# A fused attention and gated-convolution kernel: its tables split into pieces, scores of batch 0 on half the rows per head, weight loads placed between the staged loads, loads of later batches spaced

## The chip, the cores and the metric

The kernel runs on one core of a Trainium2 chip. The metric is the device time of one execution in microseconds (us). Three executions of the kernel before are known: 435.98, 435.8 and 434.76 us, median 435.8.

A core has five engines that run their own instruction queues in order and wait for each other by semaphores: TensorE (PE, matmuls), VectorE (DVE), ScalarE (ACT), GpSimd (POOL) and SyncE (SP, which here only issues transfers). Transfers are issued by SP or POOL and carried out by 16 DMA engines.

## What is computed

Attention with one added to the softmax's denominator, then a gated long convolution by Fourier transform, cut to its core:

```python
# q, k, v: (8, 12, 448, 64) float32; w_proj (768, 2304), filter_fft (448, 768), w_out (768, 768)
scores = q @ k.T / sqrt(64)
m = max(scores);  e = exp(scores - m)
attn = e / (sum(e) + exp(-m) + 1e-9)
x = (attn @ v) as (8, 448, 768)
x1, x2, x3 = split(x @ w_proj, 3)
conv = irfft(rfft(x2, axis=1) * rfft(filter_fft, axis=0))
out = (x1 * conv * x3) @ w_out          # (8, 448, 768) float32
```

## The kernel before

**Units.** The twelve heads of a batch are taken in six pairs; pairs are numbered through the batches (`i` or `g`, 0 to 47). A pair's attention (`attention(i)`) has four `scores` steps on PE into PSUM: one matmul of 448 columns for the 64 keys left over of both heads (`t` = 0), and for `t` = 1 to 3 two matmuls, one per head, each with 128 keys and all 128 rows of the two heads' features. So that a head doesn't see the other's features, POOL first spreads q into a tile `qz` that is zero in the other head's 64 rows (`spread`, two copies; three such tiles in turn, so `qz` of pair i waits for the scores of pair i-3). ACT takes the exponentials (`exps`), PE multiplies with v (`attn_out`, two halves), DVE divides (`norm`) into `xb`, and `xb` is transposed into `xT`: by PE and a DVE copy for all of batch 0 and the last pair of a batch, by a transposing DMA from SP for the others (`x_dma`).

**The dense part** (`dense(b)`) needs `xT` of all six pairs. DVE folds it (`first`, `second`: a copy of two columns, sums and differences) into `xf`; PE projects (`proj2`, eight chunks P of six matmuls with the weight part 1), turns the result into a spectrum (`spectrum`), DVE multiplies by the filter's spectrum `hrs`, PE transforms back (`inverse`); PE makes the gates x1 and x3 straight from `xT` (`gate`, weight parts 0 and 2); DVE multiplies, PE projects with `wout_bf`, ACT copies out, SP stores.

**Loads.** Batches 0 and 1 are staged (`staged(b)`): SP loads a pair's k, q and v as float32 into one of three slots of `nat`, and `rests`, the left-over keys and values, once a batch. Casts to bfloat16 follow (k and q on DVE, but q of pairs 1 to 5 on POOL; v on POOL), then PE transposes k and q (`turn`), and two copies bring them to `kT` and `qT`. Batch 1 loads q in rows of 1 KB (four sequence rows at once), and ACT puts the columns in order while it copies. Batches 2 to 7 (`loaded(b)`) are cast in the transfer by 13 DMAs from POOL, and transposed by DMAs from SP (`q_turn`, four, and `k_turn`, six a batch). They need room in `nat`, which the transposes of the batch before give.

**Weights and tables.** `wproj_bf` comes in three parts, `filt` and `wout_bf` in one each, from POOL, each at a time after a cast of some v. The Fourier tables (`tables`, `more_tables`) are written at the start outside the planner, almost all on DVE: phases, a sine on ACT, `half`, `jm`, `ft`, `bt`, and on PE and ACT the mirrored `fr`.

**What sets the order.** All work is handed to a planner (`Plan`) as tasks with an engine, a cost, a due time (`want`), what they need and make, and buffers they take and give; `after` is an earliest time. It plays the tasks through by its own costs and writes down each engine's order; on the chip nothing of the times is left, only the order and the waits. `tau(i)` is the due time of pair i, `PERIOD` 46 for a batch.

Of the kernel before, what the change touches and what calls it, by code (L numbers as in the profile page):

```python
# [11 lines left out]
AF = mybir.ActivationFunctionType  # L12
# [8 lines left out]
SP = 112  # L21
# [20 lines left out]
class Plan:  # L42
# [17 lines left out]
    def run(self):  # L60
# [14 lines left out]
        rings = {"SP": 0.0, "POOL": 0.0}  # L75
# [22 lines left out]
        while any(queue.values()):  # L98
            moved = False
            for e in queue:  # L100
# [17 lines left out]
                if dma:  # L118
                    other = rings["SP" if e == "POOL" else "POOL"]
                    begin = max(rings[e], end)  # L120
                    rings[e] = begin + dma * (1.6 if other > begin else 1.0)
                    end = rings[e] + 1.8
# [23 lines left out]
def kernel(  # L146
# [14 lines left out]
    NSTAGED = 2  # L161

# [47 lines left out]

    def stage(g, at, n):
        o = (g % 3) * SLOT + at
        return nf[:, o : o + n]
# [10 lines left out]
    ATT0, SLOT0, PERIOD = 7.5, 3.5, 46.0  # L224
    BASE = ATT0 + 6 * SLOT0

    def tau(i, frac=0.0):

        i += frac
        return ATT0 + SLOT0 * i if i < NHP else BASE + (i - NHP) * PERIOD / NHP  # L230

# [11 lines left out]
    def staged(b):  # L243


        for hp in range(NHP):
            g = b * NHP + hp
            want = tau(g) - (8.0 if b == 0 else 12.0)
            natural = b == 0
            for n, (name, x) in enumerate((("k", k), ("q", q), ("v", v))):  # L250
                src = stage(g, (0, 768, 384)[n], (384, 512, 384)[n])

                def load(name=name, x=x, src=src, hp=hp):
                    if name == "q" and natural:
# [5 lines left out]
                    elif name == "q":  # L260
                        nc.sync.dma_start(
                            src[0:SP].rearrange("p (u c) -> p u c", u=2),
                            x[b, 2 * hp : 2 * hp + 2].rearrange("u (p j) d -> p u (j d)", j=NST),
                        )
# [5 lines left out]
                add("SP", 1.0 if name == "q" and natural else 0.45, want + 0.1 * n, load, need=[("c" + name, g - 3)] if g >= 3 else (),  # L270
                    make=[("s" + name, g)],
                    dma=1.6 if name == "q" and natural else 0.8)
                if hp == 0 and name != "q":
                    add("SP", 0.45, want + 0.1 * n + 0.15,
                        lambda n=n, x=x: nc.sync.dma_start(rests[:, n // 2], shared(x, b)),
                        need=[("cr" + name, b - 1)] if b else (), make=[("r" + name, b)], dma=0.75)

                def cast(name=name, src=src, hp=hp, g=g):
                    if name == "k":
                        T[g]["kn"] = t = ld.tile([128, 3, 128], BF16, name="k0")  # L280
                        nc.vector.tensor_copy(
# [3 lines left out]
                    elif name == "q":  # L285
                        T[g]["qn"] = t = ld.tile([SP, NST, 2, DH], BF16, name="q0")
                        (nc.gpsimd if natural and hp else nc.vector).tensor_copy(
# [11 lines left out]
                if name == "v":  # L299
                    add("POOL", 0.75, tau(g) + 1.0, cast, need=[("sv", g)], make=[("cv", g), ("v", g)])  # L300
                else:
                    on_pool = name == "q" and natural and hp > 0
                    add("POOL" if on_pool else "DVE", 0.8 if on_pool else 0.45, tau(g) - (2.0 if b == 0 else 5.0), cast, need=[("s" + name, g)], make=[("c" + name, g)],
                        after=tau(g) - (4.0 if b == 0 else 7.0) if g >= 3 else 0.0,
                        take=[(name + "0", g)])
            if hp == 0:
                for u in range(2):
                    c = slice(64 * u, 64 * u + 64)
                    add("DVE", 0.25, want + 6.0, lambda c=c: nc.vector.tensor_copy(ks[c, :, c], rests[c, 0]),
                        need=[("rk", b), "zero ks"] + ([("T", NHP * b - 1)] if b else []), make=[("crk", b)])  # L310
                    add("POOL", 0.5, tau(g) + 1.0,
# [20 lines left out]
            def q_back(g=g, hp=hp):  # L332
                tb = T[g]["ps"].bitcast(BF16)
                if natural:
# [711 lines left out]
```

## Time and profile before

| | us |
|---|---|
| three executions | 434.76 to 435.98, median 435.8 |
| the profiled execution | 433.81 |
| its span, first to last instruction | 432.0 |
| PE busy | 394.7 (91%) |
| DVE, ACT busy | 274.7 (64%), 275.3 (64%) |
| POOL busy | 164.5 (38%) |

Times below are from the profiled execution, counted from the span's start. A line of the timeline gives start, duration, engine, line of the source, operation, the tiles it writes and reads, and in brackets the engine's idle time before it with what ended it. In lines of groups stand the count, the total, the mean in ns, and the idle time before. PE's clock is given as a share of full speed.

### The profile page before, as it was taken

The numbers are of one execution on the slowest core, as the hardware profiler recorded it, in microseconds if no ns is written. First come the engines' busy times: TensorE is split into PE (matmuls) and PEld (weight loads), VectorE is DVE, ScalarE is ACT, GpSimd is POOL, SyncE is SP. The second block draws the span as 40 slices with busy tenths as digits, with TensorE's granted clock in tenths as the row PEclk, the third lists the DMA queues.
The fourth block names the chain that finished last, engine by engine and source line by source line (L and its number), as shares of the span: only waits on it lengthen the run. The fifth ranks groups of instructions, "written<-read, shape, count | busy, mean of one in ns | idle before, by whom it ended". The sixth has DMA issues, their size and how long they took to land.

```text
span 432.0 us, 9027 instructions
## 1 busy us (share of the span) xinstructions
PE 394.7 (91%) x3401; PEld 262.3 (61%) x3401; DVE 274.7 (64%) x782; ACT 275.3 (64%) x460; POOL 164.5 (38%) x257
## 2 busy tenths in 40 slices
PE   1795689979898899999999999999999999999995
PEld 1463457646574566766676667666766667666562
DVE  7585546784564845787567844884689457764660
ACT  3584548747666566776767776777687666753433
POOL 7872340955657431681456234814131121000000
PEclk9998879989999899999999999999999999999999
DMA  8999971999999969992999299917970220102004
GB/s 204 215 230 231 249 139 31 107 142 159 189 143 143 102 135 149 134 122 46 203 130 114 42 177 179 139 18 145 137 79 14 86 86 14 26 14 109 3 0 146
DMA packets 178011, 51.09 MB, mean 118 GB/s; under 512 B 163373, under 2 KB 174384, under 8 KB 177968
## 3 DMA queue, kind: packets, MB, share of 16 engines
q0 software_dynamic: 101680, 17.80, 61.3%
q1 hardware_dynamic: 76288, 32.72, 39.3%
q8 instruction: 26, 0.43, 0.4%
q14 instruction: 17, 0.14, 0.1%
HBM read 43.86 MB, written 11.01 MB: 127 GB/s over the span
## 4 chain that ended last, share of the span: by engine, by line
PE 80%; DMA 8%; DVE 6%; issue 2%; ACT 2%; POOL 1%; SPq 0%; DVEq 0%; POOLq 0%; ACTq 0%
PE pps L809 22%; PE pps L736 14%; PE ops L904 12%; PE sc L583 11%; PE op L616 7%; DMA xT<-xb 5%; PE cps L843 4%; DMA nat<-in_v_dram 3%; PE op L611 2%; PE xsp L763 2%; PE sc L585 2%; ACT e L591 1%; DVE t L777 1%; PE tps L324 1%; PE xps L665 1%
## 5 line engine op out<-in xcount | busy, mean ns | idle before, releaser
L591 ACT ACTIVATE e<-sc 128x896 bf16<-128x896 f32 x144 | 129.9, 919 | 42.5 <-PE sc L583 41.6
L809 PE MATMUL pps<-xT,wproj_bf 128*128 128x448 bf16 x576 | 122.5, 353 | 1.8 <-DMA xT<-xb 1.0
L572 POOL COPY qz<-qT 64x448 bf16<-64x448 bf16 x96 | 60.9, 634 | 113.9 <-PE sc L583 82.5
L583 PE MATMUL sc<-qz,kT 128*128 128x448 bf16 x288 | 80.2, 367 | 8.7 <-POOL qz L572 8.6
L809 PEld LDWEIGHTS <-wproj_bf 128*128 128x128 bf16 x576 | 55.7, 98 | 49.8 <-issue 3.1
L736 PE MATMUL pps<-wproj_bf,xf 128*113 128x384 bf16 x384 | 72.2, 331 | 0.6 <-ACT xs L771 0.4
L616 PE MATMUL op<-vn,e 128*128 128x65 bf16 x1152 | 59.2, 195 | 0.9 <-ACT e L591 0.6
L736 PEld LDWEIGHTS <-xf 128*113 128x113 bf16 x384 | 50.7, 134 | 15.4 <-issue 1.4
L616 PEld LDWEIGHTS <-e 128*128 128x128 bf16 x1152 | 51.8, 99 | 7.8 <-ACT e L591 1.4
L904 PE MATMUL ops<-wout_bf,yT 128*128 128x384 bf16 x288 | 51.4, 326 | 0.0
L629 DVE TENSOR_SCALAR rec<-op 128x4 f32<-128x4 f32 x96 | 15.2, 158 | 56.8 <-PE op L616 56.5
L821 ACT CAST x<-pps 128x448 bf16<-128x448 f32 x48 | 25.7, 535 | 38.8 <-PE pps L809 35.7
L611 PE MATMUL op<-vr,er 128*128 128x130 bf16 x192 | 42.5, 221 | 3.7 <-DVE xb L631 3.7
L631 DVE TENSOR_TENSOR xb<-op,rec 128x256 bf16<-128x256 f32 x96 | 40.7, 424 | 3.3
L904 PEld LDWEIGHTS <-yT 128*128 128x128 bf16 x288 | 27.7, 98 | 19.1 <-issue 0.2
L777 DVE TENSOR_TENSOR t<-xs,hrs 113x768 bf16<-113x768 bf16 (+1 forms) x64 | 36.4, 605 | 4.2 <-ACT xs L771 3.9
L824 DVE TENSOR_TENSOR g<-x,pps 128x448 bf16<-128x448 bf16 x48 | 29.7, 618 | 14.2 <-PE pps L809 8.4
L583 PEld LDWEIGHTS <-kT 128*128 128x128 bf16 x288 | 24.5, 99 | 22.0 <-issue 11.9
L916 ACT COPY osb<-ops 128x384 f32<-128x384 f32 x56 | 25.9, 479 | 17.1 <-PE ops L904 16.3
L748 DVE CAST x<-pps 113x384 bf16<-113x384 f32 x32 | 17.8, 555 | 22.3 <-PE pps L736 22.3
L596 ACT ACTIVATE er<-sc 128x448 bf16<-128x448 f32 x48 | 26.4, 550 | 8.6 <-PE sc L585 8.5
L750 ACT CAST x<-pps 113x384 bf16<-113x384 f32 x32 | 15.5, 485 | 25.3 <-PE pps L736 25.2
(98 smaller groups left out, 492.1 us busy)
## 6 DMA issues: line engine op xcount, KB each, us to landing
out_dram<-osb SPq DMA_DIRECT2D x24, 384.0 KB, 2.9
nat<-in_q_dram POOLq DMA_DIRECT2D x24, 168.0 KB, 5.6
vn<-in_v_dram POOLq DMA_DIRECT2D x6, 672.0 KB, 14.2
wproj_bf<-in_moe_w_proj_dram POOLq DMA_DIRECT2D x3, 1152.0 KB, 14.8
nat<-in_k_dram POOLq DMA_DIRECT2D x36, 96.0 KB, 4.8
nat<-in_k_dram SPq DMA_DIRECT2D x12, 192.0 KB, 4.2
nat<-in_v_dram SPq DMA_DIRECT2D x12, 192.0 KB, 9.0
out_dram<-osb SPq DMA_DIRECT2D x8, 192.0 KB, 3.1
```

What stands on the lines that cost most here:

```text
L572: nc.gpsimd.tensor_copy(z[c, u, :], qT[b % 2][c, hp, :])
L583: nc.tensor.matmul(sc[:, u, 0:S], kT[b % 2][:, hp, t, :], z[:, u, :])
L591: nc.scalar.activation(e[:, 0 : 2 * S].rearrange("p (u n) -> p u n", u=2), sc[:, :, 0:S], AF.Exp, scale=SCALE)
L596: nc.scalar.activation(e[:, 0:S], sc[:, 0, 0:S], AF.Exp, scale=SCALE)
L611: nc.tensor.matmul(op[:, n, :, :], e[0][:, o : o + 128], vr[b % 2][:, hp, :, :], start=True, stop=False)
L616: nc.tensor.matmul(op[:, n, u, :], e[1 + t][:, u * S + o : u * S + o + 128], vn[b % 2][:, hp, 4 * u + t, :], start=False, stop=(u == 1 and ...
L631: nc.vector.tensor_tensor(W["xb", b][:, hp, 2 * hf : 2 * hf + 2, :].rearrange("p t (u d) -> p t u d", u=2), op[:, :, :, 0:DH], rec[:].unsq ...
L736: nc.tensor.matmul(pps[:FQ, :DCH], W["xf", b][:, pg, kt, 0:FQ], wproj_bf[:, kt, D + ch * DCH : D + (ch + 1) * DCH], start=(kt == 0), stop= ...
L777: nc.vector.tensor_tensor(t[:K], L["xs", par, ch][:K], h, op=ALU.mult)
L809: nc.tensor.matmul(p[:, :S], wproj_bf[:, kt, 2 * part * D + dt * 128 : 2 * part * D + (dt + 1) * 128], xT()[:, kt, 0:S], start=(kt == 0), ...
L824: nc.vector.tensor_tensor(g[:, dt, :], L["x1", dt], p[:, :S], op=ALU.mult)
L904: nc.tensor.matmul(ops[:n, :DCH], y[:, dt, 0:n], wout_bf[:, dt, ch * DCH : (ch + 1) * DCH], start=(dt == 0), stop=(dt == NDT - 1),)
```

## The change

- **Tables.** `tables` becomes `count`, `phases`, `sines` and `weights`, each a task of the planner. Phases stay on DVE, the sine on ACT; `half`, `jm`, `ft` and the unfolding of `bt` go to POOL. The zeros of `ks` and `vr` are written by ACT (copies of a zero column), those of `qz` and `vr[1]` by DVE. PE begins with 40 matmuls whose result is not used (`spin`).
- **Scores of batch 0** use only the 64 rows of their head in `kT` and `qT`, so batch 0 needs no `qz`; its `t` = 0 scores go to a PSUM buffer of the `hy` group.
- **Staged loads.** Both batches load q in rows of 256 B; the copies back of batch 1's q go from ACT to DVE. Batch 1 loads v first, into slots in another turn, and starts only when all v of batch 0 are cast. k of pairs 1 to 5, and q of all but pair 0, are cast on POOL.
- **Weights** are issued in the order part 1, filter, part 0, part 2, `wout`, each after a cast: of q of pair 5, the same, v of 7, v of 9, v of 11.
- **Fold of batch 0** in three pieces (3, 2 and 1 slices of `xT`) instead of two.
- **Later batches.** The 13 loads get due times 1.5 us apart, from batch 3 on also as earliest times.
- Due times and costs of the planner change with it; it counts all transfers on one line instead of two.

The diff, cut:

```diff
-    ATT0, SLOT0, PERIOD = 7.5, 3.5, 46.0
-    BASE = ATT0 + 6 * SLOT0
+    SPIN = 40
+    READY0 = 35.0
+    GATES = ((1, ("cq", 5)), ("F", ("cq", 5)), (0, ("cv", 7)), (2, ("cv", 9)), ("O", ("cv", 11)))
+    STEP = 1.5
+    ATT0, SLOT0, PERIOD = 6.0, 3.5, 46.0
+    BASE = 31.0
...
     def staged(b):
+            parts = (("k", k, 0, 384), ("q", q, 768, 512), ("v", v, 384, 384))
+            if b:
+                parts = parts[::-1]
-                    if name == "q" and natural:
+                    if name == "q":
                         for u in range(2):
                             nc.sync.dma_start(
                                 src[0:SP, 256 * u : 256 * u + 256].rearrange("p (j d) -> p j d", j=NST),
                                 q[b, 2 * hp + u].rearrange("(j p) d -> p j d", j=NST),
                             )
...
+                need = [("c" + name, slot(g))] if g >= 3 else []
+                if b:
+                    need.append(("cv", NHP * b - 1))
...
+                on_pool = name == "q" and g > 0 or name == "k" and 0 < g < NHP
+                eng = nc.gpsimd if on_pool else nc.vector
...
-            add(*(("DVE", 0.42) if natural else ("ACT", 1.2)), w + 0.1, q_back, need=[("T", g)], make=[("qT", g)], give=[hy])
+            add("DVE", 0.42, w + 0.1, q_back, need=[("T", g)], make=[("qT", g)], give=[hy])
...
     def loaded(b):
+        start = want if b > NSTAGED else 0.0
-                add("POOL", 0.85, want + 0.1 * n, lambda u=u, t=t: k_load(u, t), need=room,
-                    make=[("kn", b)], dma=1.0)
+                add("POOL", 0.85, want + STEP * n, lambda u=u, t=t: k_load(u, t), need=room,
+                    make=[("kn", b)], dma=1.0, after=start + STEP * n)
...
     def attention(i):
+        halves = b == 0
-        for u in range(2):
+        for u in range(0 if halves else 2):
             add("POOL", 0.68, tau(i) - 4.0 + 0.1 * u, lambda u=u: spread(u),
...
                 for u in range(2):
-                    nc.tensor.matmul(sc[:, u, 0:S], kT[b % 2][:, hp, t, :], z[:, u, :])
+                    c = slice(64 * u, 64 * u + 64) if halves else slice(0, 128)
+                    nc.tensor.matmul(
+                        sc[:, u, 0:S], kT[b % 2][c, hp, t, :], qT[b % 2][c, hp, :] if halves else z[:, u, :]
+                    )
...
-        for g in range(2):
+        for ds in (slice(0, 3), slice(3, 6)) if b else (slice(0, 3), slice(3, 5), slice(5, 6)):
...
+        add("PE", 4.0, -20.0, spin, need=["ident"], make=["spin"], take=[("hy", "spin")], give=[("hy", "spin")])
+        add("ACT", 1.6, -20.0, lambda: blank(ks[:].rearrange("p g c -> p (g c)")), need=["zero1"], make=["zero ks"])
```

What this does to the queues is seen at three places. First POOL, where weights are issued; `vn` are v casts, `q_` q casts, `bt` and `ft` tables, `filt` the filter, `wproj_bf` a weight part, `qT` and `qz` with 100 belong to batch 0. Before, from `qz` of pair 2 to the third weight part (the first stands one row ahead):

```order
L572 COPY qz_104<-qT_100 64x448 x2
L287 CAST q_387<-nat 112x2x4x64
L294 CAST vn_105<-nat 128x3x64 x2
L312 CAST vr_108<-rests 64x6x64 x2
L572 COPY qz_102<-qT_100 64x448 x2
L287 CAST q_467<-nat 112x2x4x64
L294 CAST vn_105<-nat 128x3x64 x2
L554 DMA wproj_bf<-in_moe_w_proj_dram 128x6x768
L572 COPY qz_103<-qT_100 64x448 x2
L287 CAST q_553<-nat 112x2x4x64
L294 CAST vn_105<-nat 128x3x64 x2
L554 DMA wproj_bf<-in_moe_w_proj_dram 128x6x768
```

Now, from the cast of q of pair 5 to the cast of v of pair 5:

```order
L300 CAST q_461<-nat 112x2x4x64
L569 DMA wproj_bf<-in_moe_w_proj_dram 128x6x768
L518 TENSOR_SCALAR ft<-sb,half 113x452
L474 DMA filt<-in_moe_filter_fft_dram 112x4x768
L475 DMA filt<-in_moe_filter_fft_dram 1x3x768
L478 DMA filt<-in_moe_filter_fft_dram 1x16x48
L513 COPY bt<-bt 113x111
L515 TENSOR_SCALAR bt<-bt 113x111 x2
L513 COPY bt<-bt 113x111
L1031 MEMSET vn_106 128x42
L1033 MEMSET vr_108 64x6 x2
L307 CAST vn_105<-nat 128x3x64 x2
```

The first weight part has moved behind the last q cast of batch 0, the filter right behind it, and the last v cast of batch 0, on which all loads of batch 1 wait, behind both. The rows that follow are v of 6, the rest of v, q of 6, v of 7, the next weight part, `qz` of 6, q of 7 and 8, v of 8 and 9, the third weight part, q of 9, `qz` of 7, v of 10, q of 10, `qz` of 8.

Second, DVE at the first projections of batch 0 (`x_` is a P chunk's copy back, `uw` the sums of the filter, 101 and 99 the tiles of batch 1). Before:

```order
L521 TENSOR_TENSOR uw<-filt 113x1536
L748 CAST x_860<-pps_872 113x384
L521 TENSOR_TENSOR uw<-filt 113x1536
L748 CAST x_860<-pps_893 113x384
L281 CAST k_910<-nat 128x2x3x64
L287 CAST q_930<-nat 112x2x4x64
L629 TENSOR_SCALAR rec<-op 128x4
```

Now, with k of pair 7 in the first row and k of pair 8 in the third:

```order
L294 CAST k_855<-nat 128x2x3x64
L536 TENSOR_TENSOR uw<-filt 113x1536
L294 CAST k_874<-nat 128x2x3x64
L773 CAST x_862<-pps_865 113x384
L345 COPY qT_101<-tps 128x448
L341 COPY kT_99<-tps 128x512
L652 TENSOR_SCALAR rec<-op 128x4
```

The cast of a k two pairs ahead now stands in front of the first copy back of P and of pair 7's `qT` and `kT`. The first `uw` has gone up DVE's queue, in front of the last two norms of batch 0.

Third, SP's transposes in batch 2 (`qT_101` and `kT_99` are of batch 3). Before:

```order
L391 DMA_TRANSPOSE qT_101<-nat 128x6x112
L655 DMA_TRANSPOSE xT<-xb 128x4x128
L391 DMA_TRANSPOSE qT_101<-nat 128x6x112 x3
L655 DMA_TRANSPOSE xT<-xb 128x4x128
L396 DMA_TRANSPOSE kT_99<-nat 128x4x128 x6
L655 DMA_TRANSPOSE xT<-xb 128x4x128 x3
```

Here the first two rows with `xT` are pairs 12 and 13, the last pairs 14 to 16. Now:

```order
L678 DMA_TRANSPOSE xT<-xb 128x4x128
L397 DMA_TRANSPOSE qT_101<-nat 128x6x112
L678 DMA_TRANSPOSE xT<-xb 128x4x128
L397 DMA_TRANSPOSE qT_101<-nat 128x6x112 x3
L678 DMA_TRANSPOSE xT<-xb 128x4x128
L402 DMA_TRANSPOSE kT_99<-nat 128x4x128 x6
```

Pair 14's transpose now stands ahead of the six `kT`. On DVE, the fold of a batch's first three slices comes after the 20th norm of the program instead of the 18th in batch 1 (there are two norms a pair, so one pair later), and one norm later in batches 2 to 6.

More of the change, by code (lines that the diff above doesn't have):

```diff
@@ L74, in run @@
         free = {e: 0.0 for e in queue}
[L75 removed]
+        dmas = 0.0
         now, order = 0.0, []
@@ L118, in run @@
                 if dma:
[L119 to L122, printed above, removed]
+                    dmas = max(dmas, end) + dma
+                    end = dmas + 1.8
                 for k in make:
```

247 lines of the change are left out of this document (131 added, 116 removed).

## The prediction

> **What bounds the kernel now.** I read the page first, then the stretches, the timelines of the stretches where TensorE (PE) is not full, and the transfers. Stretches; the columns are busy time of PE, weight loads, VectorE (DVE), ScalarE (ACT) and GpSimd (POOL), PE's granted clock, DMA share and GB/s:
>
> ```profile
> core 0: us, PE busy (x) PEld busy (x) DVE busy (x) ACT busy (x) POOL busy (x), PEclk, DMA share, GB/s
> 40.00:58.00 18.00, 10.30 (x86) 6.48 (x85) 8.38 (x26) 7.78 (x11) 9.14 (x19) 0.77 0.97 210
> 58.00:80.00 22.00, 21.80 (x182) 15.46 (x181) 14.85 (x42) 15.04 (x29) 5.46 (x9) 0.96 0.56 78
> 80.00:100.00 20.00, 17.07 (x136) 11.07 (x135) 15.65 (x36) 12.14 (x20) 13.70 (x17) 0.91 2.47 142
> 100.00:120.00 20.00, 18.38 (x181) 11.88 (x178) 8.34 (x29) 13.43 (x21) 12.73 (x15) 1.00 1.84 178
> 120.00:140.00 20.00, 18.79 (x162) 12.45 (x161) 11.89 (x31) 13.34 (x23) 12.80 (x19) 1.00 1.58 142
> 140.00:160.00 20.00, 17.86 (x148) 11.49 (x148) 14.12 (x42) 12.01 (x20) 7.98 (x12) 0.91 1.11 101
> 160.00:380.00 220.00, 219.51 (x1949) 148.67 (x1947) 150.28 (x426) 156.56 (x266) 76.18 (x102) 1.00 0.99 103
> ```
>
> From 160 to 380 PE is busy 219.5 of 220 us: nothing is to be had there unless matmuls go, and none go. The room lies before 58, where PE gets 86 matmuls done in 18 us at a clock of 0.77, and in 80 to 160. Before 58 the staged loads decide. PE waits for `qz`, and `qz` stands on POOL behind casts that wait for a load:
>
> ```profile
> 53.49 0.64 POOL L294 CAST vn<-nat 128x192 bf16<-128x192 f32 x2 [3.82 <-DMA nat<-in_v_dram]
> 54.68 0.53 PE L583 MATMUL sc<-qz,kT 128*128 128x448 bf16 x1 [3.71 <-POOL qz L572]
> ```
>
> In 80 to 160 it is the queues: DVE's fold copy (L708) waits for `xT` transposes, and what stands behind it holds PE up.
>
> ```profile
> 86.40 1.81 DVE L708 COPY xT<-xT 128x6 bf16<-128x6 bf16 x1 [1.65 <-DMA xT<-xb]
> 90.78 0.29 PE L611 MATMUL op<-vr,er 128*128 128x130 bf16 x1 [2.93 <-DVE xb L631]
> 113.02 0.17 DVE L708 COPY xT<-xT 128x6 bf16<-128x6 bf16 x1 [2.51 <-DMA xT<-xb]
> 140.85 0.17 DVE L708 COPY xT<-xT 128x6 bf16<-128x6 bf16 x1 [5.17 <-DMA xT<-xb]
> ```
>
> PE's idle time there, with the clock behind it: 80 to 100, 2.9 idle and 0.09 x 20 = 1.8 of clock, 4.7; 100 to 120, 1.6; 120 to 160, 1.2 + 2.1 + 1.8 = 5.1. Together **11.4 us**.
>
> How transfers share is in the DMA view of two windows (first line 4 to 16: staged loads alone; the others 32 to 46: weights on q0 beside staged loads on q1):
>
> ```profile
> DMA packets 8077, 3.04 MB, mean 254 GB/s; under 512 B 6029, under 2 KB 8077, under 8 KB 8077
> q0 software_dynamic: 1395, 2.12, 82.6%
> q1 hardware_dynamic: 1397, 1.10, 31.2%
> ```
>
> Staged loads alone run at 254 GB/s. Beside weights the queues take turns packet for packet, 100 a us each: a weight part (1152 KB in pieces of 1536 B, 2.12 MB over 1395, so 768 packets) takes 7.7 us there, and a staged load moves one packet for each.
>
> **The change, step by step.** Times are us from the span's start; pairs of heads are numbered through, 0 to 5 in batch 0, 6 to 11 in batch 1.
>
> *First scores.* Rows of the start, and two of pace:
>
> ```profile
> 4.99 0.63 DVE L434 SCALAR_TENSOR_TENSOR ph<-rd,ph 128x452 f32<-128x452 f32 x1
> 8.91 0.35 DVE L281 CAST k<-nat 128x384 bf16<-128x384 f32 x1
> 9.52 0.71 DVE L309 CAST ks<-rests 64x384 bf16<-64x384 f32 x2
> 10.38 0.27 PE L318 MATMUL tps<-ident_bf,ks 128*128 128x128 bf16 x1 [2.64 <-DVE ks L309]
> 12.15 0.56 PE L585 MATMUL sc<-qT,kT 128*128 128x448 bf16 x1 [0.82 <-DVE kT L330]
> 22.53 2.58 ACT L591 ACTIVATE e<-sc 128x896 bf16<-128x896 f32 x3 [0.64 <-PE sc L583]
> 26.18 2.58 ACT L591 ACTIVATE e<-sc 128x896 bf16<-128x896 f32 x3 [0.64 <-PE sc L583]
> ```
>
> Today table work fills DVE from 5.6 to 8.9; then k, q and `ks` take it 1.3, to 10.2. The table work goes to POOL or later, so the three end at 7.0, PE transposes at 7.1, and scores begin 1.8 later as now: 8.9, **3.3 us sooner**. The zeros that ACT now writes hide in its wait for the phases; the 40 spin matmuls (0.27 for one of 128 columns in L318's row, successors overlapping) lie where PE has nothing to do, and cost only what they last past 7.1. A pair then takes 3.65 (22.53 to 26.18), set by ACT's exponentials and PE between them; half-row scores stream as many columns, so I leave it (bounds 3.1, ACT's busy time, and 3.65). Six pairs end near 31.
>
> *Weights.* Rows: POOL's casts, a weight's issue, the landings of `wout` (alone) and of the three parts, the filter's sum:
>
> ```profile
> 21.47 0.61 POOL L287 CAST q<-nat 112x512 bf16<-112x512 f32 x1
> 22.03 0.63 POOL L294 CAST vn<-nat 128x192 bf16<-128x192 f32 x2
> 18.58 0.96 POOL L554 DMA_DIRECT2D wproj_bf<-in_moe_w_proj_dram  x1
> wout_bf<-in_moe_w_out_dram POOLq DMA_DIRECT2D x1, 1152.0 KB, 8.8
> wproj_bf<-in_moe_w_proj_dram POOLq DMA_DIRECT2D x3, 1152.0 KB, 14.8
> 54.34 1.09 DVE L521 TENSOR_TENSOR uw<-filt 113x1536 bf16<-113x1536 bf16 x1 [2.38 <-DMA filt<-in_moe_filter_fft_dram]
> ```
>
> Batch 0 (4.13 MB) alone takes 16.3 us at 254 GB/s and is in at 19.5; nothing shares its way any more. POOL has by then fifteen casts: five q, five v, and five k, for which it has no row (bounds: 0.35 on DVE, 0.63 for a v of the same size on POOL; I take 0.63, of the same engine). That is 9.4, with `vr` (1.1) and the weights of the tables (six small operations, without a row on POOL: 0 to 0.6 each, a cast's price, I take 0.2, since five have one column) 11.7 of the 13 us from 6.5: it fits. The first weight part (the one for `x2`) is issued at 19.5 and lands 8.8 later, 28.3. The filter's 448 packets follow. POOL comes to the last v of batch 0 only behind the weight's issue 0.96, three of the filter (under 0.96 each, I take 1.8), `ft` and four unfolding copies (no row on POOL: 0 to 0.63 each, I take 0.6 and 1.0), two memsets (0.7, no more than a cast) and its own cast 0.63: 25.2, and SP's whole batch 1 waits for that. So filter and batch 1 share from 26.8, and the filter lands near 32.5; `uw` ends at 33.6, and the last half pair and its norm stand behind it on DVE and PE.
>
> *Batch 1's first pair.* Today's norm, a q cast, the `xT` copy and the fold of three slices, end to end from 46.58 to 50.90:
>
> ```profile
> 46.58 0.16 DVE L629 TENSOR_SCALAR rec<-op 128x4 f32<-128x4 f32 x1 [0.25 <-PE op L616]
> 50.31 0.59 DVE L716 TENSOR_TENSOR xf<-w 128x339 bf16<-128x339 bf16 x2
> ```
>
> DVE's queue has k of pair 6 and `ks` ahead of that last norm. v, the rest of v, q, k and the rest of k are 992 KB; a tenth is in by 32, the rest takes 3.6 alone: 35.6. Then on DVE: `ks` 0.7; norm to fold 4.3 as quoted, the q cast standing for one of two copies back, 0.4 for the other; 0.5 less, as the first chunk needs only the sums: the projection P starts at **40.5** (today 24 of its first 30 matmuls start at 57).
>
> *The second weight part* is issued behind pair 7's v (0.8 on, 36.4; cast 0.63, issue 0.96, and 1.3 to its first packets: 0.1 if 768 packets fill 7.7 of `wout`'s 8.8, 2 if they go faster alone), and stands ahead of `qz` of pair 6 on POOL. SP has by then moved q, k of 7, v of 8 and half of q of 8. What is left, 500 packets of q (256 B each now, 896 a pair) and 256 of k, goes one for one: 7.6 us, so k of 8 lands at 48. Its cast stands on DVE ahead of P's copy back and of pair 7's `qT` and `kT`. PE runs out of work near 45.5 and goes on at 49.8: a **new wait of 4.3**, and 1.8 of clock behind it, as in 80 to 100. The third part behind v of 9 does the same to q of 10, whose cast stands ahead of `qz` of 8: ready at 59.3. From 49.8 PE has 7.1 of work (the order's columns up to there, at P's 384 in 0.16), 1.8 of clock and 0.7 for `qz` of 7 up to that point, 59.4: even.
>
> *Against today.* What PE has done by 62.8 (matmul groups of that window, and P's price from the chain):
>
> ```profile
> L583 PE MATMUL sc<-qz,kT 128*128 128x448 bf16 x46 | 15.2, 435 | 8.7 <-POOL qz L572 8.6
> L616 PE MATMUL op<-vn,e 128*128 128x65 bf16 x164 | 9.6, 200 | 0.8 <-ACT e L591 0.6
> L736 PE MATMUL pps<-wproj_bf,xf 128*113 128x384 bf16 x30 | 6.6, 383 | 0.0
> L809 PE MATMUL pps<-xT,wproj_bf 128*128 128x448 bf16 x6 | 1.3, 352 | 0.0
> 117.24 0.97 PE pps L736 x6
> ```
>
> The new order has by 59.4 done 48 such scores and one more of the first tile (3 x 0.19, 448 columns by P's rate), 180 outputs (16 more, with 2 of 130 columns, 0.6), 36 of P (0.97 more), 16 matmuls of the filter's spectrum, which today all come later (2.6 at P's 0.16 each), two more of X2's spectrum (0.3), but none of the gates (1.3 less): 3.7 us more. Today PE is full from 58, so it has as much done at 66.5. The start gives 66.5 - 59.4 = **7.1**. Bounds: 0 (the filter 6 us later, as the parts took 14.8 in place of 8.8, and qz of 8 with it) and 14 (no wait at 45).
>
> *Later queues.* The wait in the chain at 80, and SP's rows before the third:
>
> ```profile
> 80.42 5.96 DMA xT<-xb
> 125.16 9.72 SPq L396 DMA_TRANSPOSE kT<-nat  x6
> 134.99 1.21 SPq L655 DMA_TRANSPOSE xT<-xb  x1
> ```
>
> Pair 14's `xT` stood behind six `kT` (9.7 us) and landed 5.8 after it; in the new order it goes ahead of them: its 5.1 go, and `kT`, needed a pair later at the earliest, is late instead without being waited for. In batch 1 the fold stands two norms further down, a pair's time, against the 6 us that the transfer took: 4.7 go, and the norms ahead are what PE needs next. Pair 10's `xT` stays behind six `kT`: 1.6 stay. Spaced loads meet every transpose a little, 0.8 by my choice (bounds 0 and the 1.6 of that middle stall, the nearest). Sum **9.0**, bounds 0 and 11.4. The spacing itself is only an order: `qz` halves between the loads. Batch 2's loads aren't spaced at all.
>
> One rule speaks against q in 256 B pieces. The Trainium skill, DMA: Bandwidth & Descriptors, Specifications, wants 512 B at least for line rate, since smaller writes are read, changed and written. The window 4 to 16 doesn't bear it out: 6029 of its 8077 packets are smaller, and it moves 254 GB/s all the same. By the rule B below would hold, and the sum would be 10.7; by the row it stays 16.1.
>
> **Rivals.** *A: the loads eat the start.* Weights meet staged loads more than I have it, DVE waits for the filter and for k of 8 longer, and the start gives 0 to 2; the queues still give 9.0: 425.8. For it: 14.8 us as the weights' median landing today. Against: w1 now goes alone. *B: q of batch 1 in 256 B pieces runs at half its rate.* 0.9 us more for each of six pairs, 5.4, on the path to P and to `qz`: 7.1 - 5.4 + 9.0 = 10.7, 425.1. *C: the queue waits only move.* The numbers that space the loads are the planner's times, not the chip's; collisions come back elsewhere: 7.1 alone, 428.7. *D: slower.* In batches 3 to 7 a `qz` half stands behind a load that waits for room, which the previous batch's `kT` transposes give, now behind an `xT`. `qz` has three buffers, so it is written about two pairs ahead; a pair takes 8 us (1949 of 3401 matmuls in 220 us, 48 a batch), so 16 are covered; a load that waited 21 would cost 5 in each of five batches, 25 against 16.1: 444.7. It decides from a wait of 19.3 us on. Against: `kT` took 9.7 us for six.
>
> **How the numbers follow.** The profiled execution lasted 433.81 (span 432.0); 433.81 - 7.1 - 9.0 = 417.7. The median of the runs shown is 435.8, 2.0 longer, so 435.8 - 16.1 = **419.7**. Chances: forecast with gains of 11.5 to 25, 0.62; A 0.12; B 0.04; C 0.10; D 0.08; next to no change 0.04. The forecast's own bounds are 410.4 (14 + 11.4) and 424; A, B and C reach 428.7; C's own term could be some smaller, so 430. D stays out. A measurement of this kernel can tell some 0.3% (1.3 us) from no change. Faster by more: 0.88; within: 0.04; slower: 0.08.
>
> **What would show it.** Right: first L608 scores near 9; w1 landing near 28, the filter near 32.5; first P near 40; DVE idle before a k cast near 43 to 48; PE full from 60, with no wait for `xT` above 2 us in 80 to 160; and 160 to 380 shifted whole. Wrong: POOL reaching w1 well after 21 (k casts or small operations dearer than I took), PE idle past 60 for `qz`, or PE waits for `qz` after 160.

## The result and the profile after

The changed kernel takes **420.0 us** in the median of four executions (417.01 to 420.86); four of the kernel before took 434.76 to 438.25, median 435.9. The ratio is 0.9616, with a 95% interval of 0.9554 to 0.9679. The profiled execution took 420.29, span 418.5, where the one before took 433.81, span 432.0: 13.5 less, against 15.9 between the medians. Forecast were 16.1 less, 419.7.

The view by stretches of the changed kernel, columns as in the prediction:

```profile
core 0: us, PE busy (x) PEld busy (x) DVE busy (x) ACT busy (x) POOL busy (x), PEclk, DMA share, GB/s
40.00:58.00 18.00, 14.24 (x125) 10.14 (x123) 11.35 (x35) 9.31 (x17) 8.41 (x17) 0.93 1.15 220
58.00:80.00 22.00, 19.70 (x155) 12.43 (x154) 14.93 (x40) 11.68 (x21) 13.05 (x19) 0.92 1.18 145
80.00:100.00 20.00, 19.18 (x180) 12.63 (x179) 12.92 (x39) 12.88 (x23) 7.72 (x11) 1.00 1.84 150
100.00:120.00 20.00, 18.93 (x177) 13.60 (x177) 12.01 (x33) 14.22 (x23) 18.78 (x25) 1.00 1.66 172
120.00:140.00 20.00, 19.78 (x174) 12.43 (x172) 16.88 (x50) 14.88 (x25) 4.69 (x7) 1.00 1.08 109
140.00:160.00 20.00, 20.00 (x177) 13.41 (x176) 10.60 (x32) 13.19 (x22) 14.47 (x18) 1.00 1.45 167
160.00:380.00 220.00, 220.00 (x1951) 148.08 (x1950) 151.33 (x431) 154.30 (x263) 71.15 (x98) 1.00 0.91 102
```

Between 80 and 160 PE now does 708 matmuls (180 + 177 + 174 + 177) at full clock, where it did 627. Before 80 it is still not full: 2.3 us idle and a clock of 0.92 between 58 and 80. The three rows in which DVE waited for `xT` have lost their waits (L730 is the same copy):

```profile
89.71 0.16 DVE L730 COPY xT<-xT 128x6 bf16<-128x6 bf16 x1
103.49 0.17 DVE L730 COPY xT<-xT 128x6 bf16<-128x6 bf16 x1
134.48 0.16 DVE L730 COPY xT<-xT 128x6 bf16<-128x6 bf16 x1
```

What is left in the start, in the timelines of PE, DVE and POOL:

```profile
7.43 0.36 PE L608 MATMUL sc<-qT,kT 128*128 128x448 bf16 x1 [0.82 <-DVE kT L341]
21.83 1.07 POOL L569 DMA_DIRECT2D wproj_bf<-in_moe_w_proj_dram  x1
22.95 1.44 POOL L518 TENSOR_SCALAR ft<-sb,half 113x452 bf16<-113x452 bf16 x1
28.58 0.83 POOL L307 CAST vn<-nat 128x192 bf16<-128x192 f32 x2
36.06 0.96 DVE L536 TENSOR_TENSOR uw<-filt 113x1536 bf16<-113x1536 bf16 x1 [2.86 <-DMA filt<-in_moe_filter_fft_dram]
46.04 0.37 PE L761 MATMUL pps<-wproj_bf,xf 128*113 128x384 bf16 x1 [1.25 <-DVE xf L738]
52.87 0.35 PE L604 MATMUL sc<-qz,kT 128*128 128x448 bf16 x1 [1.69 <-POOL qz L587]
61.63 0.35 PE L604 MATMUL sc<-qz,kT 128*128 128x448 bf16 x1 [2.02 <-POOL qz L587]
```

Scores start sooner than forecast; the filter's sum and P come later; and PE waits twice for `qz`, which stands on POOL behind the cast of a q that has not landed.

**Landmarks.** Medians of one kernel differ by some us from one set of runs to another (the kernel before took 430.5 to 440.6 us in the comparisons below). The ratios leave out executions more than 1.5% above the fastest of the same kernel (one of the kernel before took 682.5), so a median and its ratio can disagree by 2 to 3 us. By the intervals of the ratios only q_1kb_order is clear of the changed kernel. So the experiments are read by the starts of four matmuls in the timeline of one profiled execution each: the first inverse of batch 0, and the first gate matmuls of batches 1, 2 and 3. Last column: from there to the end.

| kernel | inverse | gate 1 | gate 2 | gate 3 | to the end | median | ratio to before |
|---|---|---|---|---|---|---|---|
| before | 83.93 | 111.08 | 164.59 | 209.38 | 222.65 | 435.9 | 1 |
| changed | 81.72 | 103.25 | 151.76 | 195.91 | 222.60 | 420.0 | 0.9616 (0.9554 to 0.9679) |
| xt14_behind_kt | 80.35 | 100.90 | 149.57 | 193.71 | 222.60 | 418.7 | 0.9603 (0.9535 to 0.9670) |
| fold1_two_norms_up | 79.12 | 105.04 | 153.23 | 197.37 | 222.61 | 422.5 | 0.9700 (0.9616 to 0.9783) |
| no_spacing | 79.27 | 101.25 | 150.09 | 195.16 | 222.63 | 420.1 | 0.9627 (0.9562 to 0.9692) |
| no_spacing_xt14_behind | 81.52 | 103.22 | 152.10 | 197.17 | 222.62 | 420.5 | 0.9639 (0.9586 to 0.9692) |
| before_xt14_ahead | 82.58 | 109.95 | 158.11 | 203.50 | 224.39 | 430.1 | 0.9864 (0.9780 to 0.9949) |
| before_both_orders | 84.79 | 108.86 | 160.17 | 205.48 | 222.83 | 431.0 | 0.9888 (0.9823 to 0.9953) |
| qz_ahead | 75.26 | 98.22 | 146.88 | 191.02 | 222.61 | 417.0 | 0.9637 (0.9552 to 0.9723) |
| weights_later | 81.42 | 101.94 | 150.10 | 194.24 | 222.63 | 418.1 | 0.9669 (0.9589 to 0.9749) |
| q_1kb_rows | 75.42 | 96.70 | 144.87 | 189.01 | 222.63 | 414.2 | 0.9591 (0.9477 to 0.9704) |
| p_first | 79.98 | 100.52 | 148.73 | 192.87 | 222.62 | 417.9 | 0.9660 (0.9564 to 0.9755) |
| one_spin | 79.22 | 100.79 | 149.41 | 193.55 | 222.61 | 417.5 | 0.9570 (0.9519 to 0.9621) |
| q_1kb_order | 73.92 | 95.32 | 144.21 | 188.35 | 222.84 | 413.3 | 0.9479 (0.9436 to 0.9522) |

From gate 3 on all but one agree within 0.3 us (in before_xt14_ahead PE has one more wait there, 1.2 us). The start scatters: the five kernels whose start is the changed kernel's (it and the next four) reach the first inverse at 79.12 to 81.72, the three with the start of before at 82.58 to 84.79.

**Where the 13.5 us came from.** To the first inverse 2.2, and 1.3 more because the changed kernel has then done more (the columns of the matmuls ahead of it, at P's 0.16 us for 384, make 48.7 us against 47.4): 3.5. From there to gate 2 it takes 70.04 against 80.66, 10.6 less those 1.3: 9.3. To gate 3, 0.6; behind it nothing. Which edits gave the 3.5 of the start was not tried one by one; of them only the spin matmuls were, and they gave nothing (one_spin).

### The profile page after: what moved, and what is told of

Same layout as the page of the kernel before. It is cut to its first block, busy times and chain, and to the rows that moved or that the text cites. A ratio compares the mean times of both kernels' runs of the same rounds, so it can differ in the third digit from the quotient of the medians.

```text
span 418.5 us, 9091 instructions
## 1 busy us (share of the span) xinstructions
PE 392.8 (94%) x3441; PEld 262.5 (63%) x3441; DVE 273.2 (65%) x781; ACT 271.6 (65%) x457; POOL 161.5 (39%) x258
## 4 chain that ended last, share of the span: by engine, by line
PE 81%; DMA 8%; POOL 3%; SPq 3%; DVE 2%; issue 1%; ACT 1%; POOLq 0%; ACTq 0%
PE pps L834 26%; PE pps L761 14%; PE ops L929 13%; PE sc L604 10%; PE op L639 7%; DMA nat<-in_q_dram 5%; PE cps L868 4%; PE op L634 2%; PE xsp L788 2%; PE sc L608 2%; DMA nat<-in_v_dram 1%; SPq L268 1%; DMA nat<-in_k_dram 1%; SPq L284 1%; POOL qz L587 1%
## 5 line engine op out<-in xcount | busy, mean ns | idle before, releaser
L587 POOL COPY qz<-qT 64x448 bf16<-64x448 bf16 x84 | 51.7, 616 | 131.6 <-PE sc L604 113.8
L604 PE MATMUL sc<-qz,kT 128*128 128x448 bf16 x252 | 68.0, 352 | 6.0 <-POOL qz L587 5.2
L802 DVE TENSOR_TENSOR t<-xs,hrs 113x768 bf16<-113x768 bf16 (+1 forms) x64 | 39.0, 644 | 4.7 <-ACT xs L796 4.7
L849 DVE TENSOR_TENSOR g<-x,pps 128x448 bf16<-128x448 bf16 x48 | 29.7, 619 | 16.8 <-PE pps L834 11.8
L604 PEld LDWEIGHTS <-kT 128*128 128x128 bf16 (+1 forms) x288 | 22.6, 97 | 17.2 <-issue 8.1
L371 POOL DMA_DIRECT2D nat<-in_k_dram x36 | 29.9, 844 | 0.4 <-issue 0.4
```

Of the source, the lines that this page charges most:

```text
L371: nc.gpsimd.dma_start(kn[:, :, 1 + t, c], kr[:, :, 4 * u + t, :])
L587: nc.gpsimd.tensor_copy(z[c, u, :], qT[b % 2][c, hp, :])
L604: nc.tensor.matmul(sc[:, u, 0:S], kT[b % 2][c, hp, t, :], qT[b % 2][c, hp, :] if halves else z[:, u, :])
L802: nc.vector.tensor_tensor(t[:K], L["xs", par, ch][:K], h, op=ALU.mult)
L849: nc.vector.tensor_tensor(g[:, dt, :], L["x1", dt], p[:, :S], op=ALU.mult)
```

## The experiments

Where a kernel only moves tasks, the planner's finished order is rearranged before it is written out; a line of such a diff says which tasks move (by what they make or need) and where to. No load, copy or matmul is added by that.

### Is it the order of the transposes and the fold?

```diff
 xt14_behind_kt (of the changed kernel)
+    ('makes', ('X', 14), 'behind', ('kT', 23)),
 fold1_two_norms_up (of the changed kernel)
+    ('makes', ('fold', 1, 0, 0), 'ahead of', ('xb', 9)),
+    ('needs', ('fold', 1, 0, 0), 'ahead of', ('xb', 9)),
+    ('needs', ('fold', 1, 0, 1), 'ahead of', ('xb', 9)),
 before_xt14_ahead (of the kernel before)
+    ('makes', ('kT', 18), 'behind', ('X', 14)),
+    ('makes', ('kT', 19), 'behind', ('kT', 18)),
...
 before_both_orders: as before_xt14_ahead, and
+    ('makes', ('fold', 1, 0, 0), 'behind', ('xb', 9)),
+    ('needs', ('fold', 1, 0, 0), 'behind', ('fold', 1, 0, 0)),
+    ('needs', ('fold', 1, 0, 1), 'behind', ('fold', 1, 0, 1)),
```

> The changed kernel with one move on SP: pair 14's xT transpose stands again behind the six kT transposes of batch 3, as before the change; all other queues are as in the changed kernel. Theory Q (the prediction's: the place on SP is what gained 5.1 us): DVE's fold in batch 2 waits 4 to 5 us for that transpose, and the kernel takes about 425 us in place of 420.0. Rival R (the place matters little, since kT no longer drags): in the changed kernel the six kT were issued 1.2 to 1.3 us apart and the next xT landed 3.7 us after its issue at 133.41, so pair 14's would be issued near 132.2, land near 136, and DVE, which reached the fold at 134.48, would wait 1.5: 420 to 421.5.

> The changed kernel with one move on DVE: batch 1's first fold (copy, two sums, four differences) stands again ahead of the two norms of pair 9, as before the change. Theory Q (the prediction's: the fold two norms further down gained 4.7 us): DVE waits for pair 8's xT and PE for the norm behind it, as at 86.4 and 90.8 before: about 424.7 us. Rival R: the xT it needs landed at 83.00 in the changed kernel and DVE had nothing to do from 81.3 to 83.19 anyway, so the norm comes only the fold's own 2.6 us later, of which PE feels at most 2: 420 to 422.

> The kernel before with one move on SP: the six kT transposes of batch 3 stand behind pair 14's xT transpose instead of ahead of it. Theory Q: the 5.17 us that DVE waits at 140.85 go, with PE's idle time and half clock behind it: about 5.1 us, 430.8 us against 435.9 for the kernel before. Rival R (the wait only moves to kT, or to the next xT): within 1.5 us of 435.9.

> The kernel before with the two moves of order on which the prediction put its 9.0 us, and nothing else of the change: on SP the six kT transposes of batch 3 behind pair 14's xT, and on DVE batch 1's first fold behind the two norms of pair 9. Theory Q (these two moves are the gain between 80 and 160): 9 us less than the kernel before, some 426 to 428, with no DVE wait for xT above 2 us at either place. Rival (in this kernel the fold's place is worth less than 2, since pair 8's xT is itself late or the first P chunk of batch 1 then is): 430, as with the one move on SP alone.

**Pair 14's `xT`.** In the kernel before the move gains what was forecast: 48.16 from gate 1 to gate 2 in place of 53.51, 5.35. In the changed kernel its undoing costs nothing: 48.67 against 48.51. The rows say why; first DVE's copy (L708 or L730) in before_xt14_ahead and in xt14_behind_kt:

```profile
133.64 0.40 DVE L708 COPY xT<-xT 128x6 bf16<-128x6 bf16 x1
```

```profile
132.96 0.17 DVE L730 COPY xT<-xT 128x6 bf16<-128x6 bf16 x1 [0.77 <-issue]
```

then pair 14's transpose in the DMA view (the last number is us from issue to landing), of the kernel before (issued at 134.99) and of xt14_behind_kt (130.38):

```profile
xT<-xb SPq DMA_TRANSPOSE x1, 5.8
```

```profile
xT<-xb SPq DMA_TRANSPOSE x1, 2.5
```

Behind six `kT` in both, it takes 5.8 us in one and 2.5 in the other. Before, POOL had issued the first load of batch 4 0.3 us ahead of it, and six more followed within 5.4. In xt14_behind_kt it goes out 0.8 ahead of the first load. In these runs the place on SP matters only when it makes the transpose meet the loads.

**Batch 1's fold.** Undone, it costs 4.4: 25.92 from the first inverse to gate 1 in place of 21.53 (the other three with this start take 20.55 to 21.98, so 3.9 to 5.4). The median, 422.5, lies between the two expectations. PE's row is the old wait again, and its clock is at half behind it, from 83.8 to 90.7:

```profile
85.00 0.29 PE L634 MATMUL op<-vr,er 128*128 128x130 bf16 x1 [3.24 <-DVE xb L654]
```

In the kernel before the same move gains 3.1 (24.07 for 27.15 to gate 1) and loses it at once: gate 1 to gate 2 takes 51.31 with both moves and 48.16 with one. PE's waits of before_both_orders between 80 and 165 (total, times, longest), and DVE's copy there:

```profile
PE pps L809 <- DMA xT<-xb: 2.5, 1, 2.5
PE sc L585 <- DVE kT L330: 1.4, 1, 1.4
```

```profile
112.32 0.50 DVE L708 COPY xT<-xT 128x6 bf16<-128x6 bf16 x1 [4.04 <-DMA xT<-xb]
```

That is pair 10's `xT`, the middle wait, which the prediction let stand at 1.6. In the DMA view of before_both_orders and of the changed kernel:

```profile
xT<-xb SPq DMA_TRANSPOSE x1, 7.2
```

```profile
xT<-xb SPq DMA_TRANSPOSE x1, 2.5
```

It is issued at 105.06, 1.6 behind the first of batch 3's loads (103.48), in the one; in the other at 98.94, and the loads begin at 103.33. So the loads begin at the same time in both, and it is the transpose that has moved, by 6.1 us: the six `kT` ahead of it start at 89.89 for 95.21, and batch 2's loads, on which they wait, are issued from 71.92 on for 77.07. On POOL three pairs of `qz` copies, 3.6 us, now stand right ahead of batch 3's loads; without them the loads would begin some 0.8 us behind the transpose (an estimate, 103.33 - 3.6 against 98.94). So the fold's move pays only in a kernel where that transpose keeps clear of the loads. Both shifts are read from the rows; neither was tried alone.

### Is it the spacing?

```diff
 no_spacing (of the changed kernel)
-    STEP = 1.5
+    STEP = 0.1
-        start = want if b > NSTAGED else 0.0
+        start = -1000.0
 no_spacing_xt14_behind: as no_spacing, and
+    ('makes', ('X', 14), 'behind', ('kT', 23)),
```

> The changed kernel with the loads of batches 2 to 7 due 0.1 us apart and no earliest time, as before the change: from batch 3 on POOL issues them in blocks again, with no qz half between them, and some rows of the other engines follow; up to 100 us nothing moves. Theory (the prediction's: the spacing is only an order, and 160 to 380 is full either way): within 1.5 us of 420.0. Rival S (the spacing is what keeps transposes and loads apart and carries the gain after 100 us): 2 to 5 us slower, with PE waits for xT or qz in 100 to 160 that the changed kernel doesn't show.

> The changed kernel without the spacing of the later loads and with pair 14's xT behind the six kT, both as before the change; each alone cost nothing. Theory (the two do the same work: pair 14's transpose was late in the kernel before because it was issued 0.3 us after the first of batch 4's loads and shared the way with them): if the transpose again meets the block of loads, DVE waits 3 to 5 us for it, 423 to 425. Rival (SP has simply become earlier against PE, so the transpose is out before the loads begin either way): within 1.5 us of 420.0.

The time stays: 420.1 and 420.5. The landmarks show a small gain of the spacing at one place, 44.15 from gate 2 to gate 3 in place of 45.07 in both kernels without it: 0.9. Up to gate 2 the two are within the scatter. With the block of loads and `xT` behind `kT`, pair 14's transpose was issued at 132.21, still 1.4 ahead of the block, and DVE reached its copy without a wait:

```profile
134.77 0.69 DVE L730 COPY xT<-xT 128x6 bf16<-128x6 bf16 x1 [0.17 <-issue]
```

So the rival holds: SP runs earlier against DVE and against the loads than before the change. Its first `kT` of batch 3 was issued 12.4 us ahead of that copy here (122.41 to 134.77), and 10.5 ahead of the point where DVE began to wait in the kernel before (125.16 to 135.68). Which edit moved it was not separated.

### Why the start gave half of its term

```diff
 qz_ahead
+    ('makes', ('cq', 9), 'behind', ('qz', 7)),
+    ('makes', ('cq', 10), 'behind', ('qz', 8)),
+    ('makes', ('ck', 9), 'behind', ('kT', 8)),
 weights_later
+    ('makes', ('w', 0), 'behind', ('cq', 9)),
+    ('makes', ('w', 2), 'behind', ('cq', 10)),
 q_1kb_rows
-     q[b, 2 * hp + u].rearrange("(j p) d -> p j d", j=NST),
+     q[b, 2 * hp + u].rearrange("(p j) d -> p j d" if b else "(j p) d -> p j d", j=NST),
...
+                if b:
+                    to, of = to.rearrange("p (c j) -> p j c", j=NST), of.rearrange("p (j c) -> p j c", j=NST)
```

In p_first the order around pair 5's end is, on PE: second half output of pair 5, its transposes, the filter's first four spectra, turn of pair 6, P(0, 0); on DVE: that pair's norm ahead of the filter's first sum, then the fold's sums for P(0, ...), and the differences behind pair 6's copies.

> The changed kernel with three moves in two queues, no load moved: on POOL the casts of q of pairs 9 and 10 stand behind qz of pairs 7 and 8 instead of ahead of them, on DVE the cast of k of pair 9 stands behind pair 8's copies back. Theory S (the waits in the start are order: qz stands behind a cast whose load is starved by weights): PE's waits of 1.96 at 52.87 and 2.30 at 61.63 go, and the half clock of 63.0 to 66.4 (1.7) with them, 3 to 6 us: 414 to 417. Rival T (the loads are late for all, and the next one, v of pair 10, which landed at 56.83, or a norm behind k, is waited for instead): 418.5 to 420.5.

> The changed kernel with the issues of weight parts 0 and 2 moved down POOL's queue: part 0 behind the cast of q of pair 9, part 2 behind that of pair 10; nothing else moves. Theory W (weights take turns with the staged loads packet for packet and starve q): the second half of q of pair 9 lands near 46 instead of 51.56, PE's wait at 52.87 goes; the second wait may stay at 0 to 2, as part 0 now runs beside pairs 10 and 11; 415 to 418. Rival (the staged loads are held up by their slots or their own rate): q of 9 lands past 50 again and the time stays within 1.5 of 420.0.

> The changed kernel with q of batch 1 loaded in rows of 1 KB (four sequence rows at once) as before the change, so 224 pieces a pair for 896; DVE's copy back puts the columns in order, and its cost for that is not known (0.4 to 1.2 us each). Theory W (packet for packet): beside weights q needs a quarter of the turns, q of 9 lands by 48 and q of 10 by 55, both waits for qz go, 3 to 6 us less unless DVE's copies give back 0.5 to 2: 415 to 418. Rival (turns go by bytes): q lands as now, 420 or a little more. If pieces of 256 B are also slow by themselves, as the prediction's case B had it, q of pairs 6 and 7, which run without weights, lands sooner too.

> The changed kernel with the order around the filter rearranged on PE, DVE and ACT: the last half pair of batch 0, its norm and its xT go ahead of the filter's first sums and spectrum, and the fold's parts that the first P chunk needs go ahead of the others; the first P chunk stands ahead of pair 6's scores. Theory F (P came 5.5 us later than predicted because the filter's sum, landed at 35.9, stands on DVE ahead of the last norms and folds): P starts near 41 instead of 43.81 and 46.04, and 2 to 4 us go: 416 to 418. Rival (the time won there is waited for at qz of pair 7, which comes at 52 to 53 whatever P does): within 1.5 of 420.0.

PE's waits between 41 and 66 in the changed kernel, then in qz_ahead, in q_1kb_rows and in p_first:

```profile
PE sc L604 <- POOL qz L587: 4.5, 5, 2.0
PE pps L761 <- DVE xf L738: 1.3, 1, 1.3
```

```profile
PE pps L761 <- DVE xf L738: 0.9, 1, 0.9
PE sc L608 <- DVE kT L341: 0.3, 1, 0.3
```

```profile
PE pps L764 <- DVE xf L741: 1.4, 1, 1.4
PE sc L607 <- POOL qz L590: 0.4, 1, 0.4
```

```profile
PE sc L604 <- POOL qz L587: 4.1, 2, 3.9
```

- **qz_ahead**: with no transfer moved, the waits for `qz` are gone and the first inverse comes at 75.26, 3.9 us sooner than the soonest of the five with the same start. So order is the wait: a `qz` whose q was ready stood behind the cast of a q that had not landed. Rival T falls. (The move of k of pair 9 on DVE was not tried apart from the other two.) 1.4 of it go again behind the inverse (22.96 to gate 1 for 21.53): PE waits 2.01 at 81.17 for a `qz` that now stands behind batch 2's loads.
- **weights_later**: q of pair 9 lands in 4.5 us in place of 8.5, and the same two waits go, but the third weight part is now late. The DMA view at the issue of pair 9's two q loads, in the changed kernel, in weights_later and in q_1kb_rows:

```profile
nat<-in_q_dram SPq DMA_DIRECT2D x2, 112.0 KB, 8.5
```

```profile
nat<-in_q_dram SPq DMA_DIRECT2D x2, 112.0 KB, 4.5
```

```profile
nat<-in_q_dram SPq DMA_DIRECT2D x2, 112.0 KB, 4.2
```

and PE in weights_later, which gives the gain back:

```profile
67.26 3.93 PE L834 MATMUL pps<-xT,wproj_bf 128*128 128x448 bf16 x12 [5.21 <-DMA wproj_bf<-in_moe_w_proj_dram]
```

- **q_1kb_rows**: with the same bytes in a quarter of the pieces both waits go, and the first inverse is at 75.42. That pair 9's q lands in 4.2 us is not yet a landing beside weights: by 41.5, when the weight part has moved its first 6 packets, all but 46 of these 224 pieces have started. In the changed kernel the second of its two loads shares the way with weights, and takes 10.4 us. Pair 10's q shares it in both kernels; the DMA view at its issue, in the changed kernel and here:

```profile
nat<-in_q_dram SPq DMA_DIRECT2D x2, 112.0 KB, 15.6
```

```profile
nat<-in_q_dram SPq DMA_DIRECT2D x2, 112.0 KB, 8.6
```

  From 45 to 48 weights (q0) and staged loads (q1) move one packet for one in both kernels, whatever their size (packets, MB, share):

```profile
q0 software_dynamic: 323, 0.50, 90.8%
q1 hardware_dynamic: 319, 0.08, 21.0%
```

```profile
q0 software_dynamic: 293, 0.45, 82.1%
q1 hardware_dynamic: 293, 0.21, 29.8%
```

  DVE's copies back take 1.15 us for 0.39 (L348 there, duration in ns as least, median and most), and PE feels little of it:

```profile
L348 DVE COPY qT<-tps x5: 1147/1149/1159, 40.2 to 71.9; 128x448 bf16<-128x448 bf16 x5
```

  Without weights the size counts for less: from 36 to 40 the transfers run at 246 GB/s in the changed kernel, where 0.44 of the 0.98 MB are in pieces of 256 B, and at 275 here, rows of the views by stretches:

```profile
36.00:40.00 4.00, 2.93 (x15) 2.03 (x15) 3.82 (x10) 1.64 (x4) 2.88 (x5) 0.50 1.20 246
```

```profile
36.00:40.00 4.00, 4.00 (x31) 3.18 (x30) 3.26 (x12) 1.96 (x4) 3.48 (x7) 0.50 1.10 275
```

The Trainium skill, DMA: Bandwidth & Descriptors, says under Queues, rings and completion order that a DMA engine takes turns between queues packet by packet; the counts from 45 to 48 agree, 323 to 319 and 293 to 293. Its 512 B for line rate (Specifications) shows here as 12%, 275 over 246. If the other pieces of the mix run at 275 too, the 256 B pieces alone run at some 216 GB/s (an estimate), a fifth less and not half, as rival B had it.
- **p_first**: P starts at 40.08 instead of 43.81, and what that brings is waited for at `qz` of pair 7, 3.9 us: the first inverse, 79.98, lies within the scatter of the five. The median, 417.9, would fit theory F, but the ratio, 0.9660, shows no gain on the changed kernel's 0.9616; by the wait and the landmark the rival holds, and P was not what bounded the start.

### The spin matmuls, and the edits together

```diff
 one_spin
-    SPIN = 40
+    SPIN = 1
 q_1kb_order: q_1kb_rows, qz_ahead and p_first together
```

> The changed kernel with 1 spin matmul instead of 40. Theory (the prediction's: they cost nothing and ACT sets the pace of batch 0): PE's clock stays at half until some 11 to 15 us, and the time is within 1.5 us of 420.0. Rival (the full clock in the first 12 us is what brings the first scores from 8.9 to 7.43 and carries through): 2 us slower or more, first scores later than 8.5.

> The changed kernel with three of the edits tried before together: q of batch 1 in 1 KB rows, casts of q of pairs 9 and 10 behind qz of 7 and 8 (and k of pair 9 behind pair 8's copies), and the order in which the first P chunk of batch 0 goes first. If the gains are of separate waits: the rows took 5.8 and the P order can add what it lost to qz of pair 7 (2 to 3 us), 411 to 413. Rival (the gains overlap, or DVE's copies of 1.15 us for 0.39 become the bound near 45): 413.5 to 416.

one_spin reaches the first inverse at 79.22, inside the scatter of the five, and its ratio overlaps the changed kernel's; its median is 2.5 us lower, more than the 1.5 that the theory allowed, so the 40 may cost a little. Its first scores start at 7.71 for 7.43, and nothing speaks for the rival's gain of 2 us. **q_1kb_order takes 413.3 us**, 0.9479 (0.9436 to 0.9522) of the kernel before, better than both kernels: its interval ends below where the changed kernel's begins. The first inverse comes at 73.92, 1.5 sooner than with the rows alone. The time lies between the two expectations: the rows and the q casts take away the same two waits, and the order around P adds about half of what was hoped.

## Why the prediction was right

The time was right, 419.7 for 420.0, and so was the size of the largest term; the start's term was mis-sized, and of the mechanisms behind the queue term one was incomplete. That the time came within 0.3 us is luck: medians of one kernel scatter by more, and in the profiled pair 13.5 us went where 16.1 were forecast (420.29 for 417.7).

- **First scores** 7.43 for 8.9. The table work did leave DVE, and PE's first transposes start at 5.56 for 7.1. Six pairs ended with ACT's last exponentials at 31.75 for 31, but not at the pace forecast: 4.05 a pair for 3.65, with waits of ACT for PE where its clock was half, from 11.8 to 18.6. The sooner start hid that. It is the slowest of the ten kernels with 40 spin matmuls, which take 3.70 to 4.05; one_spin takes 3.76.
- **Weights and filter** came about 3 us late throughout: batch 0 was in at 21.1 for 19.5, and the first part, issued at 21.83, landed at 31.3 for 28.3. POOL then took 1.44 for `ft` where 0.6 was taken, the cast on which batch 1 waits began at 28.58 where its end was put at 25.2, and the filter landed at 35.9 for 32.5. First P 43.8 for 40.5. p_first shows that this was nearly free, since `qz` of pair 7 came later still.
- **The new wait of 4.3 at k of pair 8** did not come. That step failed: it took the second weight part to be ahead of k of 8. The part was issued at 40.79, 3.8 later than forecast (36.4 and a cast of 0.63), and its first packets started near 43; k of 8 landed at 44.33, where 48 was forecast (the terms given for that make 46.9: 36.4, 0.63, 0.96, 1.3 and 7.6). The mechanism, one packet for one, then took the next victim: q of pair 9 and q of pair 10, and with them `qz` of 7 and 8, which stand behind their casts; 1.96 and 2.30 of PE with their second halves, and a clock of 0.92 between 58 and 80, 1.7. The prediction had 0.7 for `qz` of 7 and saw that of 8 stand behind the cast, but ready at 59.3; it was written from 60.91 on.
- **The start's term: 7.1 forecast, 3.5 measured** in the profiled pair, and 4.9 with the middle ones of five and of three profiled executions (80.35 and 83.93). Within its bounds of 0 to 14. The 2 to 3.5 us missing are near what the wait for `qz` of 8 and the clock behind it cost, 4.0, and qz_ahead, which takes both `qz` waits away, gains 3.9 or more at the first inverse.
- **The queue term: 9.0 forecast, 9.3 measured.** Its parts were right where they stood and incomplete in their reason. The fold's place is worth 4.4 (4.7 forecast) in the changed kernel. Pair 14's place is worth 5.35 (5.1) in the kernel before, and nothing in the changed one, where the transpose gets out ahead of the loads by itself. Pair 10's wait of 1.6, which was to stay, went, and must go for the fold's part to count: before_both_orders has both moves and gains 5 to 6 us, not 9. So that the sum came out is no proof of its reasons: a gain that the sum left out stands in for one that was not there to be had. The spaced loads, which were to lose 0.8, gain 0.9.
- **160 to 380 shifted whole**: right to 0.05 us behind gate 3. No wait for `qz` behind 160, so rival D fell; PE waits there 0.0 of 220.
- **Rivals.** A's way was half true: weights do eat into the start, by their turns, not by the filter. B's way, 0.9 a pair from slow small pieces, was too large without weights and right in kind beside them, and the prediction, which rested on a stretch without weights, gave it 0.04; the 1 KB rows bring 3.7 to 6.3 us at the first inverse and 5.8 by the medians, though the intervals of the two ratios overlap. C fell: between 80 and 160 no wait of PE is left above 0.8 us.
- **Its signs.** No wait for `xT` above 2 us and the shift of 160 to 380 came. The DVE wait before a k cast came for k of pair 9, 4.17 us before 54.10, not near 43 to 48, and PE did not wait for it. PE is full from 62 and at full clock from 66.4, not from 60. And one sign of being wrong came: PE idle past 60 for `qz`, 2.30 at 61.63.

## What to carry to other kernels

Where two queues take turns by packets, look at the size of the pieces beside the other queue's, not alone: loads in small pieces starve as soon as large ones share their way. A cast that waits for a load should not stand on an in-order engine ahead of work whose input is there already; moving it moved no transfer and brought the first inverse 3.9 us ahead here. And when a wait for a transfer is taken away by reordering, try the move alone in both kernels: its worth may hang on whether the next transfer meets a block of loads.

## What was not expected of the hardware

With 40 spin matmuls PE has its full clock from 5 us on, and then loses half of it for 6.8 us. The same drop, of 3.4 to 6.8 us between 9.7 and 18.6, is in all ten profiled kernels with 40. With one spin matmul PE starts slow, and there is no drop from 15.4 to 32.5. Two stretches of the changed kernel, then of one_spin:

```profile
4.90:11.75 6.85, 4.03 (x41) 2.03 (x38) 3.20 (x9) 5.32 (x9) 3.85 (x9) 1.00 1.05 253
11.75:18.60 6.85, 6.51 (x59) 4.00 (x58) 3.79 (x14) 4.49 (x7) 4.36 (x12) 0.50 1.20 233
```

```profile
4.90:11.75 6.85, 4.70 (x24) 1.77 (x24) 3.15 (x9) 5.02 (x8) 3.86 (x9) 1.00 1.04 265
11.75:18.60 6.85, 6.78 (x84) 4.51 (x83) 4.47 (x18) 5.35 (x8) 6.05 (x17) 1.00 1.14 242
```

In the first stretch one_spin's granted clock reads 1.00 although its first score matmul takes 0.56 us (0.36 in the changed kernel): its trace has no record of the clock before 15.4, and a stretch without a record is shown as 1.00. From 4.9 to 18.6 it does 108 matmuls against 100, some of which are still spins. A transposing DMA of one `xT` took 2.5 us with the way clear and 5.8 to 8.6 beside a block of loads.
